# ScalarE's row sums as an inner register loop, and a period loop on GpSimd, in a decode attention kernel

## The chip, the cores and the metric

The kernel runs on one core of a Trainium2 chip. The metric is the time of one execution on the device, in microseconds (us); lower is better. Each version is run several times. The engines are called PE (matmul), DVE (VectorE), ACT (ScalarE), POOL (GpSimd) and SP (which issues the loads).

## The reference

Two independent attention blocks, A and B, each decode one new token against a long cache. With batch 2, 32 heads, 8192 cached positions and head size 192, each block does this:

```python
q = (x @ wq).reshape(B, Sq, H, Dh).transpose(0, 2, 1, 3)      # Sq = 1, D = 640
scores = jnp.einsum("bhqd,bhkd->bhqk", q, k_cache) * (Dh ** -0.5)
p = softmax(scores, axis=-1)
o = jnp.einsum("bhqk,bhkd->bhqd", p, v_cache)
y = o.transpose(0, 2, 1, 3).reshape(B, Sq, H * Dh) @ wo
# the result is concatenate([y_A, y_B], axis=-1), in bf16
```

Every K and V element is used once: 2 blocks x 2 x 32 heads x 2 caches x 8192 x 192 x 2 bytes = 805 MB must be read.

## The kernel before

Work goes by "units", one unit being one head of one batch entry: 128 units in all. A unit has 8192 positions as 128 partitions x 64 rows of 192 numbers. For each unit

- SP loads K and V (3.1 MB each, two buffers each);
- DVE multiplies K by q. For rows 0 to 15 the products go to `prodA`, and ACT sums each row; for rows 16 to 63 they go to `prodD`, and DVE folds and sums them itself;
- DVE takes the max of the 64 scores, POOL takes it over the partitions, ACT computes the exp, and PE multiplies by V.

The parts that the change touches:

```python
class _Stream:                       # one engine's list of operations with their waits
    ...
    def emit_part(self, eng, plan, period):
        best = self.loops(plan, period) if period else None     # finds repeats at this period
        if best is None:
            ...                                                 # emitted one by one
            return
        i0, m, n, step = best
        self.emit_part(eng, plan[:i0], period)
        with eng.bass.Fori(0, n, ...) as it:                    # the period loop
            for fn, need, has_sig, _ in plan[i0:i0 + m]:
                ...   # semaphore values are a register: it * step + val
        self.emit_part(eng, plan[i0 + m * n:], period)
...
        def act_acc(u, t):                                      # one row sum on ACT
            return lambda eng: eng.activation(prodA[u % 2][:, t, :], prodA[u % 2][:, t, :], ACTF.Identity,
                                              accum_out=sc[u % 2][:, t:t + 1])
...
            put(dve_tab, u + 1, 0, dve_d3(u), [("acc", u), ("r", u), key("ar", u - 2)], ("d3", u))   # max
            put(dve_tab, u, 2, dve_d1a(u), [("k", u), ("a0", qg_of(u)), key("acc", u - 2)], ("d1a", u))
            ...
            put(pool_tab, u + 1, 0, pool_ar(u), [("d3", u), key("nb", u - 2)], ("ar", u))
            ...
            for t in range(na_of(u)):                           # 16 rows
                w = [("d1a", u), key("d3", u - 2), key("exp", u - 2)] if t == 0 else []
                put(act_tab, u, 10 + t, act_acc(u, t), w, ("acc", u) if t == na_of(u) - 1 else None)
...
                S_pool.emit(eng)        # POOL: no period loop
...
                S_dve.emit(eng, 8)      # DVE, ACT: a loop of eight units
...
                S_act.emit(eng, 8)
...
                S_pe.emit(eng, 4)
```

Of the kernel before, what the change touches and what calls it, by code (L numbers as in the profile page):

```python
# [6 lines left out]
ACTF = mybir.ActivationFunctionType  # L7
# [95 lines left out]
def build_kernel(nc, blocks, out, cfg=None):  # L103
# [11 lines left out]
    scale = float(Dh) ** -0.5  # L115

    NA_MAIN = min(cfg.get("NA", 16), T - 2)
    LAG = cfg.get("LAG", 3)
    LATE = LAG - 1
    NPB = 4  # L120
# [14 lines left out]
    def na_of(u):  # L135
        return NA_MAIN

    NA_MAX = NA_MAIN
    ND_MAX = T - NA_MAIN

    def qg_of(u):
        blk, h, b, g = unit(u)
        return 2 * (g // 2) + b
# [4 lines left out]
    with ExitStack() as es:  # L148
# [11 lines left out]
        prodA = [sb(f"prodA{i}", [128, NA_MAX, Dh], BF16) for i in range(2)]  # L160
        prodD = sb("prodD", [128, ND_MAX, Dh], BF16)
        sc = [sb(f"sc{i}", [128, T], F32) for i in range(2)]
# [27 lines left out]
        S_pool = _Stream("pool", sem("s_pool"), reg)  # L190
# [11 lines left out]
        def key(name, *idx):  # L202
            for i in idx:
                if i < 0:
                    return None
            return (name,) + tuple(idx)
# [13 lines left out]
        def pieces(u):  # L220
            if u not in PCS:
                return None
            n0, cuts = PCS[u]
            ends = [c * T // 64 for c in cuts]
            return [(t0, t1, vtail[n0 + i]) for i, (t0, t1) in enumerate(zip([0] + ends[:-1], ends))]
# [65 lines left out]
        def pool_ar(u):  # L291
            return lambda eng: eng.partition_all_reduce(mg[u % 2][:], mp[u % 2][:], 128, bass.bass_isa.ReduceOp.max)  # L292

        def pool_ls(u):
            g, b = u // B, u % B
            return lambda eng: eng.partition_all_reduce(lall[g % 2][:, b:b + 1], rs[u % 2][:], 128,  # L296
                                                        bass.bass_isa.ReduceOp.add)
# [5 lines left out]
        def dve_d1a(u):  # L303
            na = na_of(u)
            return lambda eng: eng.tensor_tensor(prodA[u % 2][:, 0:na, :], kb[u % NK][:, 0:na, :], qb_bc(u, na), ALU.mult)  # L305

        def dve_d1b(u):
            na = na_of(u)
            return lambda eng: eng.tensor_tensor(prodD[:, 0:T - na, :], kb[u % NK][:, na:T, :], qb_bc(u, T - na), ALU.mult)  # L309

        def dve_d3(u):
            return lambda eng: eng.tensor_reduce(mp[u % 2][:], sc[u % 2][:], AXL.X, ALU.max)  # L312

        def dve_lvl(u, w):
            nd = T - na_of(u)
            return lambda eng: eng.tensor_tensor(prodD[:, 0:nd, 0:w], prodD[:, 0:nd, 0:w], prodD[:, 0:nd, w:2 * w], ALU.add)  # L316

        def dve_r(u):
            na = na_of(u)
            return lambda eng: eng.tensor_reduce(sc[u % 2][:, na:T], prodD[:, 0:T - na, 0:24], AXL.X, ALU.add)  # L320
# [2 lines left out]
            s0 = 64 * (g % 2)  # L323
            return lambda eng: eng.reciprocal(rcT[(g // 2) % 2][s0:s0 + 64, :], lall[g % 2][s0:s0 + 64, :])

        def act_acc(u, t):
            return lambda eng: eng.activation(prodA[u % 2][:, t, :], prodA[u % 2][:, t, :], ACTF.Identity,  # L327
                                              accum_out=sc[u % 2][:, t:t + 1])

        def act_nb(u):  # L330
            return lambda eng: eng.activation(nb[u % 2][:], mg[u % 2][:], ACTF.Identity, scale=-scale)  # L331

        def act_exp(u):
            return lambda eng: eng.activation(pb[u % NPB][:, :, ::32], sc[u % 2][:].rearrange("p (j a) -> p j a", a=2),  # L334
                                              ACTF.Exp, bias=nb[u % 2][:], scale=scale, accum_out=rs[u % 2][:])
# [41 lines left out]
        def pe_p0(qg):  # L377
            pr, b = qg // 2, qg % 2
            g0 = 2 * pr
            blk = g0 // Hn  # L380
            w = g0 // HG
            npr = HG // 2

            def at(slot, off):
                def fn(eng):
                    for c in range(DC):
                        ins = eng.matmul(qps[:, 0:QW], xbc[blk][b][:, c, :],  # L387
                                         wqs[:, slot, c, off].rearrange("p a n -> p (a n)") if slot is not w % 2 else
                                         wqs[:, slot, c, off],
                                         start=(c == 0), stop=(c == DC - 1))  # L390
                    return ins
                return fn
            fn = at(w % 2, slice((pr % npr) * QW, (pr % npr + 1) * QW))
            fn.same = (blk, b)
            fn.turn = lambda it: at(bass.ds((it + pr) // npr % 2, 1), bass.ds((it + pr) % npr * QW, QW))
            return fn, [("wq", w) if w == 0 else None, ("wq0b",) if (w == 0 and WQSPLIT and pr % npr >= 1) else None,
                        ("xbc", blk), key("a0", qg - 1)]

        def pe_pv(u, j0, j1):
            b = u % B  # L400
            vv = v_tile(u)[:].rearrange("p (j a) d -> p j (a d)", a=2)

            def fn(eng):
                for j in range(j0, j1):
                    ins = eng.matmul(ops[(u // B) % 2][0:33, b, 0:QW], pb[u % NPB][:, j, :], vv[:, j, :],  # L405
                                     start=(j == 0), stop=(j == T // 2 - 1))
                return ins
            fn.same = (j0, j1)
            return fn
# [45 lines left out]
        act_tab = [[] for _ in range(NSLOT)]  # L455
# [3 lines left out]
        def put(tab, slot, order, fn, waits, sig):  # L459
            tab[slot].append((order, len(tab[slot]), fn, waits, sig))  # L460

        for u in range(NU):
            g = u // B
            put(dve_tab, u + 1, 0, dve_d3(u), [("acc", u), ("r", u), key("ar", u - 2)], ("d3", u))
            put(dve_tab, u, 2, dve_d1a(u), [("k", u), ("a0", qg_of(u)), key("acc", u - 2)], ("d1a", u))
            put(dve_tab, u, 3, dve_d1b(u), [("k", u), ("kb", u) if u in KSPLIT else None, ("a0", qg_of(u)),
                                            key("r", u - 1)], ("d1b", u))
            put(dve_tab, u, 4, dve_lvl(u, 96), [("d1b", u)], ("l1", u))
            put(dve_tab, u, 5, dve_lvl(u, 48), [("l1", u)], ("l2", u))
            put(dve_tab, u, 6, dve_lvl(u, 24), [("l2", u)], ("l3", u))  # L470
            put(dve_tab, u, 7, dve_r(u), [("l3", u), key("d3", u - 2), key("exp", u - 2)], ("r", u))
            put(pool_tab, u + 1, 0, pool_ar(u), [("d3", u), key("nb", u - 2)], ("ar", u))
            put(pool_tab, u + 1, 1, pool_ls(u), [("exp", u), key("f2", g - 2)], ("ls", u))
            put(act_tab, u + 1, 0, act_nb(u), [("ar", u), key("exp", u - 2)], ("nb", u))
            put(act_tab, u + 1, 1, act_exp(u), [("nb", u), ("acc", u), ("r", u), key("pv", u - NPB)], ("exp", u))
            for t in range(na_of(u)):
                w = [("d1a", u), key("d3", u - 2), key("exp", u - 2)] if t == 0 else []
                put(act_tab, u, 10 + t, act_acc(u, t), w, ("acc", u) if t == na_of(u) - 1 else None)
            pc = pieces(u)
            w0 = [("exp", u), key("f1", g - 2), ("init",)]  # L480
            if pc is None:
                put(pe_tab, u + LATE, 0, pe_pv(u, 0, T // 2), w0 + [("v", u)], ("pv", u))
            else:
                for i, (t0, t1, sm) in enumerate(pc):
                    put(pe_tab, u + LATE, 0, pe_pv(u, t0 // 2, t1 // 2), (w0 if i == 0 else []) + [("vp", u, i)],
                        ("pv", u) if i == len(pc) - 1 else None)
# [15 lines left out]
        for pp in range(G // 2):  # L502
# [13 lines left out]
            w = [("f4", pp), key("f5", pp - 1)]  # L516
# [8 lines left out]
        for qg in range(NQG):  # L525
            fn, w = pe_p0(qg)
# [20 lines left out]
        for u in range(NU):  # L547
            korder.append(("k", u))
            lag = min(1 + u // 8, LAG)
            while u - lag >= nv:  # L550
# [4 lines left out]
        for kind, u in korder:  # L555
            if kind == "k":
# [11 lines left out]
                w = u // UG  # L568
# [27 lines left out]
        with nc.Block() as block:  # L596
            @block.sync
            def _(eng):
                S_sp.emit(eng)

            @block.gpsimd
            def _(eng):
                S_pool.emit(eng)

            @block.vector
            def _(eng):
                S_dve.emit(eng, 8)

            @block.scalar
            def _(eng):  # L610
                S_act.emit(eng, 8)

            @block.tensor
            def _(eng):
                S_pe.emit(eng, 4)
# [49 lines left out]
```

## Time and profile before

Median 1961.84 us of three runs (1961.54 to 1963.42).

| what | value |
|---|---|
| data moved | 837 MB at 427 GB/s |
| data queue, share of 16 DMA engines' span | 99.7% |
| DVE / PE / ACT / POOL busy | 84 / 57 / 46 / 9% |
| ACT's 16 row sums per unit | 5.6 us |
| span per unit (1961.8 / 128) | 15.3 us |

These are lines of the page of the kernel before. First come the DMA queues (packets, MB, share of 16 engines), then the rate in 40 slices of the span, the shares of the chain of waits that ended last, groups of instructions (count, then busy us, mean ns of one, then idle us before them and what ended it), and DMA issues (KB, us from issue to landing):

```profile
GB/s 371 429 430 431 432 430 433 431 430 433 431 433 433 429 432 433 431 433 431 432 430 431 432 430 433 431 432 428 435 432 431 432 430 433 431 432 431 432 432 299
...
q1 hardware_dynamic: 56432, 836.79, 99.7%
q8 instruction: 12, 0.20, 0.0%
q14 instruction: 16, 0.13, 0.0%
...
DMA 72%; PE 22%; DVE 5%; issue 1%; SPq 0%; ACT 0%; DVEq 0%
...
L327 ACT ACTIVATE prodA<-prodA 128x192 bf16<-128x192 bf16 x2048 | 709.0, 350 | 117.0 <-DVE prodA L305 116.8
...
L305 DVE TENSOR_TENSOR prodA<-kb,qbc 128x3072 bf16<-128x3072 bf16 x128 | 225.2, 1759 | 238.9 <-DMA kb<-in_B_k_cache_dram 126.9
L327 ACT ACTIVATION_READ_ACCUMULATOR prodA<-prodA 128x1 f32 x2048 | 386.9, 189 | 0.0
...
kb<-in_A_k_cache_dram SPq DMA_DIRECT2D x63, 3072.0 KB, 22.5
```

The reader sees a kernel limited by its loads: the queue is full from the second slice to the last but one, ACT has no share in the chain, and DVE is idle 239 us waiting for K. The rate in these slices is 428 to 435 GB/s.

One unit in the timeline of the kernel before (start us, duration us, engine, line, operation; in brackets the idle time before and what ended it):

```profile
818.20 1.76 DVE L305 TENSOR_TENSOR prodA<-kb,qbc 128x3072 bf16<-128x3072 bf16 x1 [3.64 <-DMA kb<-in_A_k_cache_dram]
...
819.99 0.36 ACT L327 ACTIVATE prodA<-prodA 128x192 bf16<-128x192 bf16 x1 [4.11 <-DVE prodA L305]
820.26 0.19 ACT L327 ACTIVATION_READ_ACCUMULATOR prodA<-prodA 128x1 f32 x1
820.35 0.34 ACT L327 ACTIVATE prodA<-prodA 128x192 bf16<-128x192 bf16 x1
...
825.44 0.18 ACT L327 ACTIVATION_READ_ACCUMULATOR prodA<-prodA 128x1 f32 x1
...
829.64 1.35 DVE L320 TENSOR_REDUCE sc<-prodD 128x48 f32<-128x1152 bf16 x1
...
831.12 0.22 DVE L312 TENSOR_REDUCE mp<-sc 128x1 f32<-128x64 f32 x1
831.43 0.35 POOL L292 PARTITION_ALL_REDUCE mg<-mp  x1 [15.08 <-DVE mp L312]
```

ACT starts 0.03 us after DVE's product ends (818.20 + 1.76 = 819.96), runs its rows every 0.345 us, and is done at 825.62. DVE wants the sums at its max, 831.12, after its own last reduction ends at 830.99. So the sums are 5.4 us early here. Over all units of this trace the smallest such lead is 2.6 us and the median 5.4 us.

### The profile page before, as it was taken

The numbers are of one execution on the slowest core, as the hardware profiler recorded it, in microseconds if no ns is written. First come the engines' busy times: TensorE is split into PE (matmuls) and PEld (weight loads), VectorE is DVE, ScalarE is ACT, GpSimd is POOL, SyncE is SP. The second block draws the span as 40 slices with busy tenths as digits, with TensorE's granted clock in tenths as the row PEclk, the third lists the DMA queues.
The fourth block names the chain that finished last, engine by engine and source line by source line (L and its number), as shares of the span: only waits on it lengthen the run. The fifth ranks groups of instructions, "written<-read, shape, count | busy, mean of one in ns | idle before, by whom it ended". The sixth has DMA issues, their size and how long they took to land.

```text
span 1961.8 us, 18371 instructions
## 1 busy us (share of the span) xinstructions
PE 1115.6 (57%) x5004; PEld 590.1 (30%) x5004; DVE 1656.0 (84%) x962; ACT 903.0 (46%) x4743; POOL 172.8 (9%) x270
## 2 busy tenths in 40 slices
PE   2445546655566555655655556556564665556657
PEld 1222223332333223322333333223332332223324
DVE  7889898888888888898888988888888888888884
ACT  4445444445444444454444444444445444544442
POOL 3013030000001000000000000000000000000000
PEclk9777777777777777777777777777777777777778
DMA  9999999999999999999999999999999999999997
GB/s 371 429 430 431 432 430 433 431 430 433 431 433 433 429 432 433 431 433 431 432 430 431 432 430 433 431 432 428 435 432 431 432 430 433 431 432 431 432 432 299
DMA packets 56476, 837.12 MB, mean 427 GB/s; under 512 B 7416, under 2 KB 18304, under 8 KB 23680
## 3 DMA queue, kind: packets, MB, share of 16 engines
q1 hardware_dynamic: 56432, 836.79, 99.7%
q8 instruction: 12, 0.20, 0.0%
q14 instruction: 16, 0.13, 0.0%
q10 hardware_dynamic: 16, 0.01, 0.0%
HBM read 836.77 MB, written 0.01 MB: 427 GB/s over the span
## 4 chain that ended last, share of the span: by engine, by line
DMA 72%; PE 22%; DVE 5%; issue 1%; SPq 0%; ACT 0%; DVEq 0%
DMA vb<-in_B_v_cache_dram 35%; DMA vb<-in_A_v_cache_dram 29%; PE ops L405 22%; DMA kb<-in_A_k_cache_dram 8%; DVE prodD L309 3%; DVE prodD L316 1%; DVE prodA L305 0%; DVE sc L320 0%; PE oTps L414 0%; PE oTps L425 0%; PE outps L441 0%; SPq L242 0%; SPq L249 0%; DVE mp L312 0%; ACT oTzL L359 0%
## 5 line engine op out<-in xcount | busy, mean ns | idle before, releaser
L405 PE MATMUL ops<-vb,pb 128*33 128x384 bf16 x4032 | 939.9, 408 | 774.1 <-DMA vb<-in_B_v_cache_dram 387.5
L405 PEld LDWEIGHTS ops<-vb,pb 128*33 128x33 bf16 x4032 | 473.4, 120 | 1231.5 <-DMA vb<-in_B_v_cache_dram 405.8
L327 ACT ACTIVATE prodA<-prodA 128x192 bf16<-128x192 bf16 x2048 | 709.0, 350 | 117.0 <-DVE prodA L305 116.8
L309 DVE TENSOR_TENSOR prodD<-kb,qbc 128x9216 bf16<-128x9216 bf16 x128 | 633.7, 4951 | 3.6 <-DMA kb<-in_A_k_cache_dram 3.6
L316 DVE TENSOR_TENSOR prodD<-prodD 128x4608 bf16<-128x4608 bf16 (+2 forms) x384 | 599.0, 1560 | 13.3
L305 DVE TENSOR_TENSOR prodA<-kb,qbc 128x3072 bf16<-128x3072 bf16 x128 | 225.2, 1759 | 238.9 <-DMA kb<-in_B_k_cache_dram 126.9
L327 ACT ACTIVATION_READ_ACCUMULATOR prodA<-prodA 128x1 f32 x2048 | 386.9, 189 | 0.0
L331 ACT ACTIVATE nb<-mg 128x1 f32<-128x1 f32 x128 | 25.9, 203 | 737.0 <-POOL mg L292 737.0
L292 POOL PARTITION_ALL_REDUCE mg<-mp x128 | 56.3, 440 | 1637.5 <-DVE mp L312 1637.5
L320 DVE TENSOR_REDUCE sc<-prodD 128x48 f32<-128x1152 bf16 x128 | 173.2, 1353 | 4.4
L296 POOL PARTITION_ALL_REDUCE lall<-rs x128 | 105.6, 825 | 114.7 <-ACT pb L334 114.7
L387 PE MATMUL qps<-wqs,xbc 128*128 (+1 forms) x320 | 67.9, 347 | 53.4 <-ACT qbc L365 42.4
L414 PEld LDWEIGHTS oTps<-ones,o_sb 33*128 33x128 f32 x372 | 67.1, 258 | 9.8 <-issue 9.8
L414 PE MATMUL oTps<-ones,o_sb 33*128 33x1 f32 x372 | 69.8, 311 | 0.0
L341 ACT ACTIVATE o_sb<-ops 1x384 f32<-1x384 f32 x63 | 29.9, 475 | 86.0 <-PE oTps L414 75.5
L365 ACT ACTIVATE qbc<-qps 128x384 bf16<-128x384 f32 x64 | 31.3, 488 | 77.4 <-PE qps L387 76.7
L334 ACT ACTIVATE pb<-sc,nb 128x64 bf16<-128x64 f32 x128 | 52.2, 408 | 16.6 <-ACT nb L331 8.3
L387 PEld LDWEIGHTS qps<-wqs,xbc 128*128 128x128 bf16 x320 | 27.2, 101 | 88.7 <-ACT qbc L365 44.3
L312 DVE TENSOR_REDUCE mp<-sc 128x1 f32<-128x64 f32 x128 | 28.2, 220 | 13.7 <-issue 4.7
L441 PE MATMUL outps<-wos,oTz 128*4 (+1 forms) x186 | 31.1, 304 | 15.1 <-ACT oTz L359 15.1
L342 ACT ACTIVATE o_sb<-ops 1x384 f32<-1x384 f32 x63 | 30.3, 481 | 0.7
L334 ACT ACTIVATION_READ_ACCUMULATOR pb<-sc,nb 128x1 f32 x128 | 23.8, 186 | 0.0
(27 smaller groups left out, 78.1 us busy)
## 6 DMA issues: line engine op xcount, KB each, us to landing
vb<-in_A_v_cache_dram SPq DMA_DIRECT2D x64, 3072.0 KB, 22.2
kb<-in_B_k_cache_dram SPq DMA_DIRECT2D x64, 3072.0 KB, 23.0
kb<-in_A_k_cache_dram SPq DMA_DIRECT2D x63, 3072.0 KB, 22.5
vb<-in_B_v_cache_dram SPq DMA_DIRECT2D x60, 3072.0 KB, 22.8
wos<-in_A_wo_dram SPq DMA_DIRECT2D x8, 960.0 KB, 26.8
wqs<-in_B_wq_dram SPq DMA_DIRECT2D x8, 960.0 KB, 24.5
wos<-in_B_wo_dram SPq DMA_DIRECT2D x8, 960.0 KB, 26.8
wqs<-in_A_wq_dram SPq DMA_DIRECT2D x7, 960.0 KB, 24.5
```

Of the source, the lines that this page charges most:

```text
L292: return lambda eng: eng.partition_all_reduce(mg[u % 2][:], mp[u % 2][:], 128, bass.bass_isa.ReduceOp.max)
L296: return lambda eng: eng.partition_all_reduce(lall[g % 2][:, b:b + 1], rs[u % 2][:], 128, bass.bass_isa.ReduceOp.add)
L305: return lambda eng: eng.tensor_tensor(prodA[u % 2][:, 0:na, :], kb[u % NK][:, 0:na, :], qb_bc(u, na), ALU.mult)
L309: return lambda eng: eng.tensor_tensor(prodD[:, 0:T - na, :], kb[u % NK][:, na:T, :], qb_bc(u, T - na), ALU.mult)
L316: return lambda eng: eng.tensor_tensor(prodD[:, 0:nd, 0:w], prodD[:, 0:nd, 0:w], prodD[:, 0:nd, w:2 * w], ALU.add)
L320: return lambda eng: eng.tensor_reduce(sc[u % 2][:, na:T], prodD[:, 0:T - na, 0:24], AXL.X, ALU.add)
L327: return lambda eng: eng.activation(prodA[u % 2][:, t, :], prodA[u % 2][:, t, :], ACTF.Identity, accum_out=sc[u % 2][:, t:t + 1])
L334: return lambda eng: eng.activation(pb[u % NPB][:, :, ::32], sc[u % 2][:].rearrange("p (j a) -> p j a", a=2), ACTF.Exp, bias=nb[u % 2][:], ...
L365: return lambda eng: eng.activation(qbc[qg % 4][:], qps[:, 0:QW].rearrange("p (a d) -> p a d", a=2), ACTF.Identity)
L387: ins = eng.matmul(qps[:, 0:QW], xbc[blk][b][:, c, :], wqs[:, slot, c, off].rearrange("p a n -> p (a n)") if slot is not w % 2 else wqs[:, ...
L405: ins = eng.matmul(ops[(u // B) % 2][0:33, b, 0:QW], pb[u % NPB][:, j, :], vv[:, j, :], start=(j == 0), stop=(j == T // 2 - 1))
L414: ins = eng.matmul(oTps[:, 2 * i + b:2 * i + b + 1], o_sb[:, b, :, :].rearrange("p s (r i) -> p i (s r)", i=3)[:, i, :], ones33[:], start= ...
```

## The change

The intent is a shorter program: ACT's 16 row sums of a unit become five passes of a register loop with three rows each, plus one row written out, and POOL gets the period loop that the other engines have. The operations, the data and the order of dependences stay.

```diff
+    ROWS = 3
...
-        def act_acc(u, t):
-            return lambda eng: eng.activation(prodA[u % 2][:, t, :], prodA[u % 2][:, t, :], ACTF.Identity,
-                                              accum_out=sc[u % 2][:, t:t + 1])
+        def act_acc(u):
+            na = na_of(u)
+            nl = (na - 1) // ROWS * ROWS
+
+            def fn(eng):
+                pa, s = prodA[u % 2], sc[u % 2]
+
+                def one(row, col):
+                    return eng.activation(row, row, ACTF.Identity, accum_out=col)
+                with eng.Fori(0, nl - ROWS + 1, ROWS) as i:
+                    for k in range(ROWS):
+                        one(pa[:, bass.ds(i + k, 1), :], s[:, bass.ds(i + k, 1)])
+                for t in range(nl, na):
+                    ins = one(pa[:, t, :], s[:, t:t + 1])
+                return ins
+            return fn
...
-            for t in range(na_of(u)):
-                w = [("d1a", u), key("d3", u - 2), key("exp", u - 2)] if t == 0 else []
-                put(act_tab, u, 10 + t, act_acc(u, t), w, ("acc", u) if t == na_of(u) - 1 else None)
+            put(act_tab, u, 10, act_acc(u), [("d1a", u), key("d3", u - 2), key("exp", u - 2)], ("acc", u))
...
-                S_pool.emit(eng)
+                S_pool.emit(eng, 8)
```

## The prediction

> **What bounds the kernel now.** The DMA queue. The page's queue part gives the one data queue 99.7% of 16 engines' span, 837 MB at 427 GB/s; 38 of 40 slices move 428 to 435 GB/s. The chain of waits is 72% DMA, 22% PE (value matmuls, whose end frees a V buffer), 5% DVE, about 0% ACT. K and V loads land 22 to 23 us after issue (DMA issues), although one 3.1 MB load needs only some 7.3 us at 430 GB/s (an estimate from those numbers): about three are in flight, so the queue does not run dry when one is issued some us late.
>
> **ACT's row sums now.** By the groups, each of 2048 rows is an ACTIVATE (350 ns) and an accumulator read (189 ns), overlapped; in the timeline rows follow every 345 ns, 16 rows in 5.6 us per unit (one head and batch; 15.3 us of span). DVE needs them only for its max, after its own last reduction; over the 128 units they are ready 2.6 us (smallest) to 5.4 us (median) before that reduction ends. DVE itself waits 239 us for K (waits), 1.9 us per unit.
>
> **What the change does.** No byte, row, buffer or dependence changes; the same 4096 ACT engine instructions run. Per unit, 15 rows become five passes of three register-addressed rows. Added per pass: three fused register operations, a register add, a compare-and-branch; per unit an entry branch, which now carries the wait for DVE. The trace of before has such instructions in the outer loops: on ACT fused register operations take 37 to 60 ns, adds 35 ns, the branch 45 ns. [...] The sequencer runs them ahead of the engine: adds in before fall within rows without moving the 345 ns pitch. A pass has about 0.24 us of control against 1.04 us of engine work.
> - Hidden (expected): sums stay 5.6 to 6.0 us per unit.
> - Not hidden at all: 5 x 0.24 = 1.2 us more, 6.9 us, still under the smallest slack.
>
> GpSimd: the 256 reductions are unchanged; register adds fall in its 13 us waits for DVE. The program gets shorter, but the instruction queues move 0.33 MB of 837 MB: nothing to win. [...]
>
> **On the critical path:** about nothing. Predicted 1962 us, 8 in 10 within 1957 to 1970. Chances: faster by over 2% 0.01, within 2% 0.95, slower by over 2% 0.04.
>
> **What would show it.** Right: data queue above 99%, slices near 430 GB/s, DVE's max not waiting for ACT, pitch 345 ns inside a pass, at most 0.3 us more at the branch, ACT busy near 46%. Wrong: DVE's max waiting on ACT in most units, larger gaps between passes, K loads issued late enough to thin the slices.
>
> **What would make it wrong.** A register-addressed activation or the branch emptying ACT's pipeline for over 0.5 us per pass; [...] start and end stalls of several us.

The forecast's sum was the time of before (1961.84 us) and about nothing on the critical path, so 1962 us, 8 in 10 within 1957 to 1970. The 0.24 us per pass comes from the records of the trace (three of 37 to 60 ns, 35 and 45 ns are 0.19 to 0.26 us). The 0.5 us per pass named as a limit is an estimate: five passes of it are 2.5 us, about the smallest lead of 2.6 us.

## The result, and the profile after

Median 1961.62 us of four runs (1957.80 to 1965.17), beside 1961.69 us for four runs of the kernel before. The ratio is 0.9998, with a 95% interval of 0.9975 to 1.0021: the same. The ratios were worked out by machine from the fast runs of the same rounds, so they are not quite the ratios of the medians quoted.

The lines of the page of the changed kernel that answer to those above, in the same columns:

```profile
GB/s 348 419 431 430 433 430 431 433 431 432 431 433 433 430 432 432 430 433 431 433 430 432 432 430 432 432 430 432 432 433 430 434 428 433 433 432 431 433 430 324
...
q1 hardware_dynamic: 56432, 836.79, 99.8%
q8 instruction: 12, 0.20, 0.0%
q14 instruction: 11, 0.09, 0.0%
...
DMA 72%; PE 22%; DVE 4%; issue 1%; SPq 0%; ACT 0%; DVEq 0%
...
L335 ACT ACTIVATE prodA<-prodA (+1 forms) x2048 | 709.2, 349 | 132.8 <-DVE prodA L306 132.5
...
L306 DVE TENSOR_TENSOR prodA<-kb,qbc 128x3072 bf16<-128x3072 bf16 x128 | 225.3, 1760 | 240.8 <-DMA kb<-in_B_k_cache_dram 126.6
L335 ACT ACTIVATION_READ_ACCUMULATOR prodA<-prodA (+1 forms) x2048 | 386.3, 189 | 0.0
...
kb<-in_A_k_cache_dram SPq DMA_DIRECT2D x63, 3072.0 KB, 22.4
```

The same work, the same queue, the same waits. The only count among these lines that moved is that of the instruction packets, 11 on queue 14 instead of 16. The timeline of one unit of the changed kernel:

```profile
820.09 1.76 DVE L306 TENSOR_TENSOR prodA<-kb,qbc 128x3072 bf16<-128x3072 bf16 x1 [3.65 <-DMA kb<-in_A_k_cache_dram]
...
822.07 0.36 ACT L335 ACTIVATE prodA<-prodA  x1 [4.40 <-DVE prodA L306]
822.34 0.19 ACT L335 ACTIVATION_READ_ACCUMULATOR prodA<-prodA  x1
822.43 0.35 ACT L335 ACTIVATE prodA<-prodA  x1
...
827.52 0.19 ACT L335 ACTIVATION_READ_ACCUMULATOR prodA<-prodA 128x1 f32 x1
...
831.53 1.35 DVE L321 TENSOR_REDUCE sc<-prodD 128x48 f32<-128x1152 bf16 x1
833.01 0.22 DVE L313 TENSOR_REDUCE mp<-sc 128x1 f32<-128x64 f32 x1
833.33 0.35 POOL L293 PARTITION_ALL_REDUCE mg<-mp  x1 [15.18 <-DVE mp L313]
```

The sums take 5.64 us again (822.07 to 827.71), with no gap at the passes: the median distance from row to row is 345 ns at every place in the unit but the first, across branches too (from the first row to the second it is 361 ns, before and after). What did change is the start: 0.22 us after DVE's product ends (820.09 + 1.76 = 821.85), where it was 0.03 us. In the trace the wait for DVE now sits on a register record at the loop's entry (a MOVE of 29 ns, at 821.88 in this unit), and a fused register operation of 78 ns follows it before the first row. No branch is recorded there: 640 of the 656 branch records of ACT are the five per unit, and the trace of before has the other 16. So the sums are 5.2 us early in the median unit instead of 5.4; the smallest lead is 2.7 us.

Register and branch instructions are not counted as busy, but the trace records them. This is one pass in the sequencer of ACT in the changed kernel (start us, duration ns, record; the notes at the right are mine, and it is a listing from the packed trace, not a view of the profile):

```
791.335  78  FUSED_REGOPS    row 1 of the pass
791.500  74  FUSED_REGOPS    row 2
791.661  74  FUSED_REGOPS    row 3
791.822  35  ALU_OP          i += 3
791.885  45  COMPARE_BRANCH  back to the next pass
792.040  78  FUSED_REGOPS    row 1 of the next pass
```

In the traces of before and after, ACT's branch records last 38 to 54 ns and PE's 208 ns in the median. A record is not the whole cost: here the next record starts 155 ns after the branch's start. A pass takes the sequencer 0.705 us when it may run freely; the engine needs 3 x 0.345 = 1.035 us for its three rows. The sequencer was more than a pass ahead by the end of a unit: its last branch record of that unit starts at 794.157, and the last of the looped rows began at 795.703.

### The profile page after: what moved, and what is told of

Its sections match the earlier page's. It is cut to its first block, busy times and chain, and to the rows that moved or that the text cites. A ratio compares the mean times of both kernels' runs of the same rounds, so it can differ in the third digit from the quotient of the medians.

```text
span 1962.7 us, 21953 instructions
## 1 busy us (share of the span) xinstructions
PE 1114.8 (57%) x5004; PEld 589.9 (30%) x5004; DVE 1656.1 (84%) x962; ACT 904.7 (46%) x4743; POOL 178.9 (9%) x270
## 3 DMA queue, kind: packets, MB, share of 16 engines
q1 hardware_dynamic: 56432, 836.79, 99.8%
## 4 chain that ended last, share of the span: by engine, by line
DMA 72%; PE 22%; DVE 4%; issue 1%; SPq 0%; ACT 0%; DVEq 0%
DMA vb<-in_B_v_cache_dram 36%; DMA vb<-in_A_v_cache_dram 29%; PE ops L419 22%; DMA kb<-in_A_k_cache_dram 8%; DVE prodD L310 3%; DVE prodD L317 1%; DVE prodA L306 0%; DVE sc L321 0%; PE oTps L428 0%; PE oTps L439 0%; PE outps L455 0%; SPq L243 0%; SPq L250 0%; DVE mp L313 0%; ACT oTzL L373 0%
## 5 line engine op out<-in xcount | busy, mean ns | idle before, releaser
L335 ACT ACTIVATE prodA<-prodA (+1 forms) x2048 | 709.2, 349 | 132.8 <-DVE prodA L306 132.5
L335 ACT ACTIVATION_READ_ACCUMULATOR prodA<-prodA (+1 forms) x2048 | 386.3, 189 | 0.0
L297 POOL PARTITION_ALL_REDUCE lall<-rs x128 | 111.6, 872 | 113.3 <-ACT pb L348 113.3
L348 ACT ACTIVATE pb<-sc,nb 128x64 bf16<-128x64 f32 x128 | 52.3, 409 | 15.1 <-ACT nb L345 5.2
```

The source lines that it names most:

```text
L297: return lambda eng: eng.partition_all_reduce(lall[g % 2][:, b:b + 1], rs[u % 2][:], 128, bass.bass_isa.ReduceOp.add)
L335: return eng.activation(row, row, ACTF.Identity, accum_out=col)
L348: return lambda eng: eng.activation(pb[u % NPB][:, :, ::32], sc[u % 2][:].rearrange("p (j a) -> p j a", a=2), ACTF.Exp, bias=nb[u % 2][:], ...
```

## The experiments

Three questions were left. Is "no change" one of two parts that cancel? Is a cost hidden under the full DMA queue? And how much could ACT be slowed before it shows? Theory A is the prediction's: control runs in the sequencer ahead of ACT's engine, and the loads set the time. The rivals are B (the change costs or gains something that the queue hides or that reaches the time), C (the parts cancel) and D (a small real difference lost in scatter). Twelve kernels ran.

### The change once more, and its two parts

The changed kernel without edit, in five rounds:

> The changed kernel once more, in five rounds, for a narrower interval. Theory A (the added control runs in ACT's sequencer ahead of its engine, and the DMA queue sets the time): ratio 0.999 to 1.001. Rival C (a cost on ACT and a gain on GpSimd cancel): the same here, and only the two part kernels differ. Rival D (the wider spread of the first four runs, 1957.8 to 1965.2, hides a real difference): a ratio clearly off 1, by 0.002 or more, with an interval that excludes 1.

ACT's loop alone:

```diff
 # the changed kernel
-                S_pool.emit(eng, 8)
+                S_pool.emit(eng)
```

> ACT's inner register loop alone, GpSimd unrolled as before. Theory A: ratio 0.999 to 1.001, row sums 5.6 us per unit, rows every 345 ns. Rival C: slower than before by over 3 us.

POOL's loop alone:

```diff
 # the kernel before
-                S_pool.emit(eng)
+                S_pool.emit(eng, 8)
```

> GpSimd's period loop alone, ACT's rows unrolled as before. Theory A: ratio 0.999 to 1.001; GpSimd's reductions begin within 0.1 us of DVE's max as before. Rival C: faster than before by over 3 us.

| kernel (five runs each, same chip) | median us | range us | ratio to before | 95% interval |
|---|---|---|---|---|
| before (nine runs) | 1961.88 | 1960.04 to 1967.94 | | |
| both parts | 1963.34 | 1961.25 to 1968.03 | 1.0017 | 0.9999 to 1.0035 |
| ACT's loop alone | 1962.15 | 1957.32 to 1964.36 | 0.9993 | 0.9974 to 1.0011 |
| POOL's loop alone | 1961.66 | 1959.96 to 1962.53 | 0.9997 | 0.9981 to 1.0012 |

Neither part alone moves the time by even 0.1% by its ratio. C needed ACT's loop to cost over 3 us, and its interval ends at 1.0011 (2.2 us), so C falls at the size it was stated in. The traces agree: ACT's loop alone has the sums of 5.64 us, the rows every 345 ns and the start 0.22 us after the product; with POOL's loop alone the start is 0.03 us as before, and POOL's reductions begin 0.09 us after DVE's max in both. "Both parts" was outside my band of 0.999 to 1.001, with an interval that just includes 1, so D isn't shown. The section on scatter below shows two sources of that size in the traced runs; only one run of each kernel was traced, so the slower runs of this table are not explained singly.

### One row per pass

```diff
 # the changed kernel
-    ROWS = 3
+    ROWS = 1
```

> One row per pass instead of three: 15 branches per unit instead of 5. Read from the changed kernel's trace, the sequencer needs 0.161 us per row, 0.063 us from the add to the branch and 0.155 us from the branch to the next pass, so 0.38 us for a pass of one row, over the engine's 0.345 us. Theory A: now the sequencer sets the pace, rows every 0.37 to 0.40 us, sums 5.9 to 6.4 us per unit, and the time still does not move (ratio 0.998 to 1.002), since DVE needs the sums 5.2 us (median) later. Rival B (small ACT costs reach the time): 128 times 0.5 us, some 60 us slower, ratio 1.03.

In most units the rows now come every 376 ns instead of 345, and the sums take 6.08 us: the sequencer sets the pace, at the size read off the trace of the three-row loop (0.38 us). The median is 1957.64 us (1957.63 to 1959.08), ratio 0.9981 (0.9966 to 0.9996). So ACT's sums got 0.44 us longer in most units and the time did not rise. Rival B's 60 us did not come. In two units of this trace (the fifth and the last) a pass took 531 and 550 ns instead of 376, 15 passes long; why is not known. There, too, the sums were in time, by 2.2 us at least. Both units lie outside the period loop and have their own copy of the code.

### Nearly no row sums at all

```diff
 # the kernel before
-            for t in range(na_of(u)):
-                w = [("d1a", u), key("d3", u - 2), key("exp", u - 2)] if t == 0 else []
+            for t in range(na_of(u) - 1, na_of(u)):
+                w = [("d1a", u), key("d3", u - 2), key("exp", u - 2)]
...
+        for i in range(2):
+            S_act.add((lambda i: (lambda eng: eng.memzero(sc[i][:, 0:NA_MAIN])))(i))
```

> The kernel before with 15 of 16 row sums taken out (their scores stay zero, so the result is wrong on purpose): about 5.2 us of ACT work per unit, 660 us of its busy time, is gone. Theory A (ACT is off the critical path): ratio 0.997 to 1.000; at most the last stretch changes, by some 2 us. Rival B (ACT's row sums reach the time): faster by over 2%.

ACT's busy time fell from 903 to 240 us, and the median was 1958.49 us (1957.66 to 1964.58), ratio 0.9984 (0.9967 to 1.0001). The result passed the comparison all the same, presumably because zeros in place of 15 of 64 scores per partition hardly shift a softmax over scores this small. Taking away 660 us of work from ACT gains some 3 us; by the interval 6.5 us at most, and perhaps nothing. A change to how these sums are issued can hardly gain more than that.

### How much slower may ACT get?

Empty register loops in front of each pass add control and no engine work:

```diff
 # the changed kernel; N = 4, 8 or 12
                 with eng.Fori(0, nl - ROWS + 1, ROWS) as i:
+                    with eng.Fori(0, N, 1):
+                        pass
                     for k in range(ROWS):
```

> The changed kernel with an empty register loop of 4 turns in front of the three rows of each pass: control alone is added, no engine work. I expect some 0.6 to 1.1 us more per pass, so the sequencer, not the engine, sets the pace: sums of 7.5 to 10 us per unit instead of 5.6. Theory A with slack as I read it: DVE's max waits for ACT in the units with the least slack, the time stays (ratio 0.998 to 1.004). Rival B: 128 times 2 to 4 us, ratio 1.12 to 1.3.

> The same with 8 turns: sums of some 10 to 14 us per unit. DVE's cycle then is its first product (1.8 us), the sums S and the max with its gaps (about 0.6 us), so S + 2.4 us against the 15.1 us that the loads give per unit. Below S = 12.5 us the time should still stay (ratio under 1.01), though DVE's max waits for ACT in nearly every unit; above it, about 128 x (S + 2.4) + 30 us.

> The same with 12 turns: sums S of some 14 to 19 us per unit. Theory A: now ACT sets the time, about 128 x (S + 2.4) + 30 us, so 2150 to 2770 us with the S that the trace shows, and the DMA queue falls clearly under 99%.

(The 0.6 to 1.1 us per pass expected of 4 turns was my estimate. In the pass listed above, it is 0.063 us from the add to the branch and 0.155 us from the branch to the next record, so 0.218 us a turn and 0.87 us for four, if a turn is an add and a branch.)

"Sums" is the time from the first row's start to the last row's end; "start" is from the end of DVE's product to the first row; the cycle is from one product of DVE to the next. All three are medians over the units of the trace (the cycle of the first two rows is the mean, as it swings with the loads).

| empty turns | sums us | start us | cycle us | data queue | median us | ratio to before |
|---|---|---|---|---|---|---|
| 0 (the change) | 5.64 | 0.22 | 15.1 | 99.8% | 1961.62 | 0.9998 |
| 4 | 7.89 | 1.12 | 15.1 | 99.8% | 1960.46 | 0.9992 (0.9974 to 1.0010) |
| 8 | 11.33 | 2.71 | 16.1 | 96.5% | 2091.37 | 1.0669 (1.0650 to 1.0688) |
| 12 | 14.77 | 3.57 | 20.4 | 77.6% | 2632.02 | 1.3419 (1.3397 to 1.3441) |

From 4 to 8 and from 8 to 12 turns a pass grows from 1.60 to 2.46 to 3.32 us: 0.215 us for each empty turn. With 4 turns ACT's sums are 2.3 us longer per unit and start 0.9 us later, 400 us over the 128 units, and nothing of it reaches the time. I had expected DVE's max to wait for ACT in some units; it didn't, the smallest lead was 0.38 us. (In this trace one unit in eight, always the same place in the eight-unit loop, spent 0.13 us more per pass. So the cost of a pass can depend on which copy of the code runs; the cause is not shown.) This is the clearest evidence against B: what the change added in the start (0.19 us) is a small part of what ACT may lose.

With 8 turns my number failed. I expected the time to stay while the sums were under 12.5 us; they were 11.3 us and the time rose by 6.7%. Two terms were missing from my cycle. The empty loop before the first pass is not in "sums": 8 x 0.215 = 1.7 us. And another 0.7 us came from POOL. This is the timeline of the kernel with 8 turns:

```profile
1010.30 0.22 DVE L313 TENSOR_REDUCE mp<-sc 128x1 f32<-128x64 f32 x1 [2.96 <-ACT prodA L335]
1010.44 1.75 DVE L306 TENSOR_TENSOR prodA<-kb,qbc 128x3072 bf16<-128x3072 bf16 x1
1010.62 1.78 POOL L293 PARTITION_ALL_REDUCE mg<-mp  x1 [9.39 <-DVE mp L313]
1012.11 4.95 DVE L310 TENSOR_TENSOR prodD<-kb,qbc 128x9216 bf16<-128x9216 bf16 x1
1012.43 0.20 ACT L347 ACTIVATE nb<-mg 128x1 f32<-128x1 f32 x1 [2.26 <-POOL mg L293]
1012.75 0.41 ACT L350 ACTIVATE pb<-sc,nb 128x64 bf16<-128x64 f32 x1
...
1014.80 0.36 ACT L335 ACTIVATE prodA<-prodA  x1 [1.62 <-issue]
```

DVE now waits for ACT (393 us in all, before its max), so K is there when the max is done, and DVE's next product starts at once: DVE is idle 2.9 us before these products in the whole run, where it was 239 us in before. POOL's reduction over the partitions then takes 1.78 us instead of 0.35 us, about as long as that product, and ACT's next steps wait for it. In the trace of before, the 8 reductions that met such a product took 1.78 us in the median, and the other 120 took 0.35 us each; here 127 of 128 meet one. In both traces such a reduction ends 0.21 us after the product's end, in the median, so it looks held until the product is done. (Spans on POOL are rough in these profiles, but ACT's step that needs the reduction starts 0.03 us after its end in both.) The cycle closes: product 1.75, start 2.71, sums 11.33, the max 0.13 us later and the next product 0.14 us after that make 16.06, against 16.1 measured. With 12 turns the same sum is 1.75 + 3.57 + 14.77 + 0.27 = 20.36, against 20.4 measured; my expected 128 x (14.77 + 2.4) + 30 = 2228 us was low by the same two terms.

That the overlap with the product causes the delay was tested next; by what mechanism it does was not shown.

### Making DVE wait for POOL

```diff
 # the kernel with 8 empty turns
-            put(dve_tab, u, 2, dve_d1a(u), [("k", u), ("a0", qg_of(u)), key("acc", u - 2)], ("d1a", u))
+            put(dve_tab, u, 2, dve_d1a(u), [("k", u), ("a0", qg_of(u)), key("acc", u - 2), key("ar", u - 1)], ("d1a", u))
```

> The kernel with 8 empty turns, which came out at 2091 us, with one more wait: DVE's first product of a unit is held back until GpSimd's max over partitions of the unit before is done. Theory P (in the kernel with 8 turns DVE starts that product at once, its K being there, and GpSimd's reduction then takes 1.78 us instead of 0.35 us, so ACT's exp and the next sums start late): the reduction takes 0.35 us again, ACT starts the sums some 0.3 to 0.5 us earlier in the cycle, and the added wait makes the kernel faster, 2030 to 2065 us, ratio to the kernel with 8 turns 0.97 to 0.99. Rival Q (the late start is the empty loop itself or ACT's queue): DVE's start is put off by 0.5 us per unit, so about 60 us slower, 2150 us.

The group of that reduction in the kernel with 8 turns, then the groups of the reduction and of DVE's product in the kernel that holds DVE back:

```profile
L293 POOL PARTITION_ALL_REDUCE mg<-mp x128 | 227.0, 1773 | 1201.2 <-DVE mp L313 1201.2
```

```profile
L306 DVE TENSOR_TENSOR prodA<-kb,qbc 128x3072 bf16<-128x3072 bf16 x128 | 225.0, 1758 | 63.7 <-POOL mg L293 61.0
...
L293 POOL PARTITION_ALL_REDUCE mg<-mp x128 | 44.8, 350 | 1721.9 <-DVE mp L313 1721.9
```

DVE waits 61 us for POOL that it did not wait before, POOL's reduction is back at 350 ns, and the kernel is faster: median 2069.18 us against 2091.37, ratio to before 1.0543 (1.0504 to 1.0582) against 1.0669. The two ran on different chips, so they are compared through the kernel before. Rival Q (2150 us) falls; P holds, though the time fell just outside its range: the gain was 22 us where I gave at least 26 (the two ratios to the kernel before give 0.988, inside the 0.97 to 0.99). ACT's start after the product went from 2.71 to 1.98 us, close to 0.22 plus 8 x 0.215 = 1.94. The hold itself puts the product off by 0.56 us (from 0.14 to 0.70 us after the max begins), so some 0.2 us per unit are left (the mean cycle went from 16.13 to 15.94). Little of this is at work in the changed kernel: there, as in the kernel before, DVE waits for K after its max, and in 120 of 128 units POOL's reduction meets no product and takes 0.35 us.

### Taking the DMA limit away

```diff
 # the kernel before, and the changed kernel
-                return dma(v_tile(u)[:], src, vsem[u % NV])
+                th = T if u < NV else T // 2
+                return dma(v_tile(u)[:, 0:th, :], src[:, 0:th, :], vsem[u % NV])
```

> The kernel before with only the first half of each V block loaded from the third unit on (except the last four; wrong result on purpose): 640 MB or so instead of 837, so the loads need under 1520 us and DVE should set the time, 12.9 us of its work per unit plus gaps. 1690 to 1750 us, ratio 0.86 to 0.89.

> The changed kernel with the same halved V loads. Theory A (ACT's sums are as quick as before but for some 0.2 us of entry, with microseconds of slack at DVE's max): within 0.2% of the kernel before with halved loads. Rival B (the change costs something that the full DMA queue hides): slower than that one by 0.2 us per unit or more, 25 us, 1.5%.

Both give a wrong result. Lines of the two pages, first the kernel before, then the changed one, both with halved V loads (engines' busy us and share; data queue):

```profile
PE 1103.6 (65%) x5004; PEld 585.0 (34%) x5004; DVE 1644.8 (96%) x962; ACT 888.4 (52%) x4743; POOL 733.0 (43%) x270
...
q1 hardware_dynamic: 56432, 644.90, 93.2%
```

```profile
PE 1111.9 (65%) x5004; PEld 587.7 (34%) x5004; DVE 1644.7 (96%) x962; ACT 888.1 (52%) x4743; POOL 740.0 (43%) x270
...
q1 hardware_dynamic: 56432, 644.90, 93.1%
```

DVE is now the limit, at 96%. The medians are 1708.57 us (1708.11 to 1708.77) and 1712.32 us (1708.14 to 1716.09), ratios to the kernel before 0.8700 (0.8669 to 0.8731) and 0.8726 (0.8690 to 0.8763). The two intervals overlap, the medians differ by 0.22%, a hair over the 0.2% that theory A gave, and the 25 us of rival B are excluded. In the traces DVE's mean cycle is 13.134 and 13.129 us, and the spans are 1707.0 and 1706.3. So in its traced run, the fastest of four, the changed kernel costs nothing per unit under a DVE limit either. Two of its four runs were 6 to 8 us longer than the other two, and that was not seen in a trace, so a difference of that size stays open. POOL's busy time of 733 us, against 173 before, is the collision described above, present here in the kernel before too: the max over partitions takes 222 us instead of 56, and POOL's other reduction (of the exp's sums) 500 us instead of 106, 3.9 us each in the mean. That is about what it takes when it meets DVE's 4.95 us product for rows 16 to 63: in the trace of before the 8 of them that began during one took 4.03 us in the median and ended 0.24 us after it, and the other 120 took 0.38 us in the median.

### The scatter of a few microseconds

The traces show two things at the ends of the span that make 2 to 7 us and are not the change's intent.

At the start, in some executions, each 24,576-byte data packet takes 1020 or 1048 ns for a while, where it takes 912 ns in the rest of these DMA-bound spans: until about 32 us in the profiled run of before, 56 us in that of the changed kernel, 72 us in that of ACT's loop alone, and not at all in those of POOL's loop alone and of one row per pass. Here is a window of 30 us near the start, for the changed kernel and then for the kernel with one row per pass (the last two columns are the DMA share and GB/s):

```profile
core 0: us, PE busy (x) PEld busy (x) DVE busy (x) ACT busy (x) POOL busy (x), PEclk, DMA share, GB/s
20.00:50.00 30.00, 6.76 (x32) 3.52 (x32) 27.38 (x15) 12.45 (x70) 9.06 (x5) 0.88 1.01 378
```

```profile
20.00:50.00 30.00, 7.79 (x32) 3.86 (x32) 29.45 (x17) 12.93 (x70) 14.16 (x5) 0.87 1.00 433
```

The engines are busy in both, and move 378 or 433 GB/s. That is 30 x (1 - 378 / 433) = 3.8 us in this window alone. Of the 6.9 us between the profiled spans of these two kernels (1962.7 and 1955.8) most is already lost by 100 us. The slow stretch comes with the kernel before as well, and what sets it is not known: one row per pass was quick in all five runs, and five runs are too few to call that the kernel's doing.

At the end, what the loads lose against 432 GB/s grows after 1900 us by 3.9 to 4.0 us in the traces of before and of POOL's loop alone, and by 1.4 to 1.9 us in the six traces with ACT's rows looped or left out in the last units (worked out from the landing times and sizes of the data packets; how the packets at 1900 us are counted moves these by up to 0.5 us, not the gap between the groups). Nearly all of it is lost in the last 5 us before the last load lands: there the rate falls in 1 us steps through 298, 129, 58, 25 and 25 GB/s in the kernel before, and through 412, 409, 310, 209 and 83 in the changed one. As 25 GB/s is about a sixteenth of 412, it looks as if the last of the 16 DMA engines finish after the others, and later in the kernel before; which engine, and why, these traces do not tell. The fastest run of the kernel before was 1960.04 us in 26 fast runs, that of five kernels with short ACT code was 1957.3 to 1957.8 us, which fits. The idea that fewer instruction packets (16 against 10 to 12 on queue 14) do it was tried with the register loop in the first eight units only:

```diff
 # the kernel before, with the looped act_acc beside it as act_acc_loop
+            if u < 8:
+                put(act_tab, u, 10, act_acc_loop(u), [("d1a", u), key("d3", u - 2), key("exp", u - 2)], ("acc", u))
-            for t in range(na_of(u)):
+            for t in range(na_of(u) if not (u < 8) else 0):
```

> The kernel before with the register loop of rows only in the first eight units, before the period loop. In the kernels so far, what the loads lose against 432 GB/s after 1900 us is 3.9 to 4.0 us where ACT's last units are unrolled and 1.4 to 1.9 us where they are looped. Theory T1 (the number of instruction packets, 16 against 10 to 12, does it): in between or short, with some 13 packets. Theory T2 (only the unrolled last units do): 3.7 to 4.2 us as before. Time as before, ratio 0.997 to 1.003.

It had 15 packets and lost 2.9 us after 1900 us, between the two groups: that leans to the packets (T1) and against T2. But T1 as stated expected some 13 packets, it is one trace, and how a packet would cost this is not shown. Its median was 1966.22 us, ratio 1.0047 (0.9976 to 1.0119), with one run at 1986.49 us. This 0.1% stays open.

## Why the prediction was right

- **The loads set the time.** Shown: the queue stayed at 99.8%, and removing ACT's sums gained some 3 us (6.5 at most), while making them 2.3 us longer per unit cost nothing that 4 runs could see. With half of most V loads cut, the kernel before fell to 1708.57 us. That the number came out within 0.4 us of 1962 is luck: the four runs of the changed kernel lie 7 us apart.
- **The control hides in the sequencer.** Shown: row distance 345 ns inside and between passes, sums 5.64 us (5.6 to 6.0 predicted). A term was mis-sized without consequence: the fused register operations with a register-addressed row take 74 to 78 ns (1888 of 1920), not 37 to 60, so a pass has 0.31 us of control records, not 0.24, and with the gaps between the records 0.705 us of sequencer time in all against the engine's 1.035. With one row per pass the sequencer does become the limit, at 376 ns a row.
- **The entry.** The prediction put the wait for DVE on an entry branch and gave no cost per unit for it. The trace has a register MOVE there instead of a branch, and the sums start 0.19 us later. It has no effect, since the sums lead by 2.7 us at least.
- **Slack.** The smallest lead of 2.6 us was right as read. As a limit for the time it may be too cautious: a lead of zero would only make DVE wait, and DVE has idle time of its own, 239 us before its products in before (this is argued; no run lies between 4 and 8 turns). The time broke between 4 and 8 empty turns, where the whole cycle passed the loads' 15.1 us per unit.
- **"Wrong if over 0.5 us per pass".** This limit was too strict: 0.56 us more per pass (4 turns) did not break it, 1.4 us more (8 turns) did.
- **A shorter program: nothing to win.** True within 2 us; some 2 us at the end that go with shorter ACT code are seen and not explained. The start and end stalls of several us that could have made the prediction wrong do not show in ACT's rows: in no unit of the changed kernel's trace does a row begin more than 0.364 us after the one before it.
- **GpSimd's loop:** nothing, as predicted; its max over partitions still takes 0.35 us in 120 of 128 units.

No kernel tried beats the kernel before by 2%; the best was one row per pass, 0.19% faster.

## What to carry to other kernels

Before costing a change on an engine, ask how long that engine may be late before anyone waits, and then how long that waiter may be late: here ACT could lose 3 us per unit for nothing (the kernel with 4 turns), since DVE came for the sums later still. Compare, too, what a pass of a register loop gives the engine with what the sequencer needs to issue it: here the loop was free at 1.035 against 0.705 us, and set the pace with one row per pass (376 instead of 345 ns). When an engine does become the limit, waits that had been harmless can collide, as POOL's reduction did with DVE's product (1.78 us instead of 0.35 us), and then an added wait can make the kernel faster (ratio to before 1.0543 instead of 1.0669).
